# Fetching a and b from ScalarE's queue, moving one exact addition to VectorE, and a fixed order for an attention and rational-FFN kernel

## Chip, core and metric

The kernel runs on one core of one Trainium2 chip. The metric is the device time of one execution in microseconds (us), as the median of several executions. A core has five instruction streams: TensorE (PE in the profile, PEld for its weight loads), VectorE (DVE), ScalarE (ACT), GpSimd (POOL) and SyncE (SP), which here issues nearly all DMAs. Each works off its own list in the order in which it was written; they meet at semaphores.

## What is computed

Two softmax attentions run one after the other, and a feed-forward layer with a rational activation follows. Cut to what matters:

```python
def _attn_ref(q, k, v, p):                  # q, k, v: 8 x 8 x 576 x 64, p: 8 x 8 x 32 x 64
    p_packed = sm_attn(p, k, v)             # 32 packed rows ask 576 keys
    return sm_attn(q, p_packed, p_packed)   # 576 queries ask the 32 packed rows

def _moe_ref(x, w_in, w_out, a, b):         # x: 4608 x 512, w_in: 512 x 2048, w_out: 2048 x 512
    h = x @ w_in
    P = a[0] + a[1] * h + a[2] * h**2 + a[3] * h**3
    Q = 1.0 + abs(b[0]) * abs(h) + abs(b[1]) * h**2
    return (P / (Q + 1e-06)) @ w_out
```

w_in and w_out arrive as 64-bit floats. a holds four numbers and b two.

## The kernel before, in words

The work of the FFN is cut into 128 units: eight batches, each in two halves of 288 tokens, each of those with eight pieces of 256 hidden columns. For one unit TensorE makes two `h` tiles (weights folded with the packed attention in `m`, times the attention weights in `AH`), ScalarE makes three functions of each from PSUM (`Y`, `U`, `sq`), VectorE multiplies up the polynomial, GpSimd adds `U` and `sq`, ScalarE takes a logarithm and an exponential into `V`, VectorE joins them into `gh` (and `gl`), and TensorE adds their products with w_out into the two `acc` banks. The first twelve units and the whole first batch use plain 32-bit matmuls; later ones use split pairs.

Before a piece of weights can be used, its 64-bit words are turned into 32-bit floats. `convert()` does it for one pair of 512 KB transfers: two ScalarE ACTIVATEs of 128x1024, two VectorE bit operations (`TENSOR_SCALAR` and `SCALAR_TENSOR_TENSOR`, 128x1024) and one exact integer addition. That addition alternates between VectorE (even pairs, CUSTOM_DVE in the profile, ISA in the order) and GpSimd (odd pairs, TENSOR_TENSOR). Sixteen pairs are converted. Raw words lie in the buffers `m` and `w`, results in `win`, `w` and `half`.

`constants()` fetches a and b into the tile `ab` with two tiny broadcast DMAs on SyncE's queue, scales them into `abS`, and works out a square root in the tile `root`: about a dozen VectorE operations on 128x1, two ScalarE ACTIVATEs, and four loads of a number into a ScalarE register (TENSOR_LOAD). Units need these before their first `Y`, `U` and `sq`.

The kernel isn't written in the order in which it runs. Every operation goes into a list, and a `Planner` with costs for each operation and each hand-over sorts the list (`order()`, by `schedule()` run forwards and backwards in several rounds); `pin()` keeps the first transfers in the order in which they stand. In `idle()` the kernel also puts small filler matmuls (operand `zero`, 64x96, added into an open `acc` bank, line L288 in the profile) where the planner sees TensorE wait before 150 us of its own reckoning. So a change anywhere can move instructions on all engines.

Everything that the planner issues has line L291 in the profile; groups are told apart by the names of their tiles.

```python
(nc.gpsimd if converted % 2 else nc.vector).tensor_add(dst.bitcast(I32), hi, di)
```

Of the kernel before, what the change touches and what calls it, by code (L numbers as in the profile page):

```python
# [15 lines left out]
I32 = mybir.dt.int32  # L16
# [7 lines left out]
P = 128  # L24
# [3 lines left out]

S = 2.0**-40


class Planner:
# [26 lines left out]
    FIRST = {"tensor": 700.0, "vector": 800.0, "scalar": 2000.0, "gpsimd": 1400.0, "sync": 700.0}  # L59
    ROUNDS = 6  # L60
    SWITCH = 95
    SLACK = 60, 100, 150, 220, 300
    IN_FLIGHT = 8
# [4 lines left out]
    def __init__(self, nc):  # L68
        self.nc, self.ops, self.pinned = nc, [], 0

# [23 lines left out]
    def cost(self, engine, name, args, kwargs):  # L94
        if engine == "sync":
            return self.DMA_ISSUE
# [39 lines left out]
    def shares(self, engine, calls):  # L136

        if engine == "gpsimd":
            return True
        if engine != "vector":  # L140
            return False
        name, args, _ = calls[0]
        aps = [x for x in args if isinstance(x, bass.AP)]
        if any(x.space == PSUM for x in aps):
            return False
        wide = sum(self.columns(x) > 8 for x in aps[1:])
        return wide > 1 or name in ("tensor_scalar", "tensor_copy")

# [42 lines left out]

    def schedule(self, before, after, rank, back=0):

        n = len(rank)
        need = [len(x) for x in before]
        at, start, end = [0.0] * n, [0.0] * n, [0.0] * n
        soon = {e: [] for e in self.ENGINES}
        ready = {e: [] for e in self.ENGINES}
        free = dict.fromkeys(self.ENGINES, 0.0) if back else dict(self.FIRST)
        port = {"vector": 0.0, "gpsimd": 0.0}  # L200
        mode, landed, dma = None, [], 0.0
        for i in range(n):
            if not need[i]:
                heapq.heappush(soon[self.ops[i][0]], (0.0, rank[i], i))
        now = 0.0
        left = n
        while left:
            for e in self.ENGINES:
                while soon[e] and soon[e][0][0] <= now:
                    heapq.heappush(ready[e], heapq.heappop(soon[e])[1:])  # L210
                if free[e] > now or not ready[e]:
                    continue
                if e == "sync" and not back and len(landed) >= self.IN_FLIGHT and landed[-self.IN_FLIGHT] > now:
                    free[e] = landed[-self.IN_FLIGHT]
                    continue
                _, i = heapq.heappop(ready[e])
                left -= 1
                s = now
                if e == "tensor" and not back and self.modes[i] != mode:
                    s += self.SWITCH  # L220
                    mode = self.modes[i]
                if not back and self.shared[i]:
                    s = max(s, port["vector" if e == "gpsimd" else "gpsimd"])
                    port[e] = s + self.costs[i]
                start[i] = s
                end[i] = free[e] = s + self.costs[i]
                if e == "sync":
                    if back:
                        dma = max(dma, end[i]) + self.transfers[i]
                        end[i] = dma + self.DMA_START + self.DMA_END - self.DMA_ISSUE  # L230
                    else:
                        dma = max(dma, s + self.DMA_START) + self.transfers[i]
                        end[i] = dma + self.DMA_END
                        landed.append(end[i])
                for j in after[i]:
                    need[j] -= 1
                    f = self.ops[j][0]
                    way = self.WAY.get((f, e) if back else (e, f), self.PASS)
                    way += back * (way > 0)
                    at[j] = max(at[j], end[i] + way)  # L240
                    if not need[j]:
                        heapq.heappush(soon[f], (at[j], rank[j], j))
            now = min(
                t
                for e in self.ENGINES
                for t in ([free[e]] if ready[e] else [max(soon[e][0][0], free[e])] if soon[e] else [1e12])
            )
        return start, end

    def order(self):  # L250
        n = len(self.ops)
        self.costs = [self.price(*x) for x in self.ops]
        self.transfers = [self.transfer(calls[0][1]) if engine == "sync" else 0 for engine, calls in self.ops]
        self.shared = [self.shares(*x) for x in self.ops]
        self.modes = [self.mode(*x) for x in self.ops]
        before = self.edges()
        after = [[] for _ in range(n)]
        for i, x in enumerate(before):
            for j in x:
                after[j].append(i)  # L260
        first = self.schedule(before, after, list(range(n)))
        best = None
        for slack in self.SLACK:
            start, end = first
            for r in range(self.ROUNDS):
                s, e = self.schedule(after, before, [-x for x in end], slack)
                m = max(e)
                rank = [m - x for x in e]
                rank[: self.pinned] = range(-self.pinned, 0)
                start, end = self.schedule(before, after, rank)  # L270
                if best is None or max(end) < best[0]:
                    best = self.best = max(end), start, end
        self.end, self.start = best[0], best[1]
        self.deps, self.t0 = dict(enumerate(before)), best[1]
        return sorted(range(n), key=lambda i: (best[1][i], i))

    def pin(self):

        self.pinned = len(self.ops)

# [42 lines left out]
def attention_rational_ffn(  # L323
# [171 lines left out]
    def convert():  # L495
# [354 lines left out]
    M = {}  # L850
# [112 lines left out]
    def acc_block(u, i):  # L963
# [160 lines left out]
```

## Time and profile before

| | |
|---|---|
| median of 3 runs | 777.11 us (776.41 to 777.18) |
| the profiled execution's own time | 776.27 us |
| its span from first to last instruction | 774.5 us |
| PE, DVE, ACT, POOL busy | 740.3, 687.1, 653.0, 473.2 us |
| moved from and to memory | 56.03 MB |

The span is 1.8 us shorter than the profiled execution's time; that part lies around the instructions. Busy time is a mean over very different stretches: in the first 60 us weights, keys and queries come in and the first batch's attention runs; until about 150 us the remaining words are converted beside the first units; then comes a long even stretch, and an end of some 20 us. A row of a timeline gives start, duration, engine, line, operation, tiles written and read, and in brackets how long the engine sat idle before it and what ended that.

### The profile page before, as it was taken

To read this page: it belongs to the slowest core of one execution; us is meant where nothing else is said; L and a number is where in the kernel's file an instruction comes from. 1 tells how busy PE (TensorE), PEld (TensorE's weight loads), DVE (VectorE), ACT (ScalarE), POOL (GpSimd) and SP (SyncE) were. 2 spreads that over 40 slices of the span, in tenths; PEclk is the share of its full clock that TensorE was granted. 3 is DMA by queue.
4 is the path that set the end of the run, shared out by engine and by line. 5 is a ranking of instruction groups with operands and counts; after the bars stand their busy time and mean duration, and the time that the engine had idled before them with its cause. 6 is when DMAs were issued, how large, how long until landed. Compare 5 with 4: busy or idle time off the path is not lost.

```text
span 774.5 us, 14987 instructions
## 1 busy us (share of the span) xinstructions
PE 740.3 (96%) x5332; PEld 568.4 (73%) x5332; DVE 687.1 (89%) x1289; ACT 653.0 (84%) x1465; POOL 473.2 (61%) x456
## 2 busy tenths in 40 slices
PE   2779999999999999999999999999999999999997
PEld 2445554588778887778788887778788887868885
DVE  4899999998999889998999889998999889998863
ACT  5789988999887898889886898989887898898872
POOL 1143568876695557756686556755686556866663
PEclk9879999999999999999999999999999999999999
DMA  9992630204601155023701155023701141000001
GB/s 299 338 372 76 193 41 0 85 29 55 104 1 56 44 68 91 1 87 48 111 1 55 45 55 104 2 86 41 117 1 55 42 57 35 1 2 28 28 0 41
DMA packets 152171, 56.03 MB, mean 72 GB/s; under 512 B 122272, under 2 KB 141472, under 8 KB 152096
## 3 DMA queue, kind: packets, MB, share of 16 engines
q1 hardware_dynamic: 151856, 54.81, 31.0%
q8 instruction: 42, 0.69, 0.4%
q14 instruction: 33, 0.27, 0.1%
q10 hardware_dynamic: 240, 0.26, 0.1%
HBM read 45.62 MB, written 9.44 MB: 71 GB/s over the span
## 4 chain that ended last, share of the span: by engine, by line
PE 68%; DVE 16%; DMA 7%; ACT 4%; issue 2%; POOL 2%; SPq 1%; ACTq 0%; DVEq 0%; POOLq 0%
PE acc L291 35%; PE h L291 20%; PE at L291 12%; DVE Y L291 8%; DMA w<-in_moe_w_in_dram 2%; DMA m<-in_moe_w_in_dram 2%; DVE V L291 2%; DVE kx L291 2%; DVE m L291 2%; DVE small L291 2%; DMA w<-in_q_dram 1%; SPq L291 1%; ACT Y L291 1%; POOL gl L291 1%; DVE w L291 1%
## 5 line engine op out<-in xcount | busy, mean ns | idle before, releaser
L291 POOL TENSOR_TENSOR U<-U,sq 128x576 f32<-128x576 f32 x128 | 185.4, 1449 | 94.6 <-ACT sq L291 47.3
L291 PE MATMUL acc<-w,gh 128*128 128x512 f32 x736 | 235.7, 406 | 0.7 <-DVE G L291 0.4
L291 PE MATMUL h<-AH,m 128*128 128x288 f32 x1024 | 199.5, 317 | 4.0 <-DVE Y L291 3.5
L291 PEld LDWEIGHTS h<-AH,m 128*128 128x128 f32 x1024 | 161.2, 189 | 46.5 <-DVE Y L291 24.5
L291 POOL TENSOR_TENSOR gl<-Y,gh 128x512 fp32r<-128x512 f32 x116 | 150.3, 1296 | 45.0 <-ACT gh L291 22.8
L291 PEld LDWEIGHTS acc<-w,gh 128*128 128x128 f32 x736 | 132.6, 188 | 38.7 <-issue 9.1
L291 ACT ACTIVATE Y<-h,abS 128x288 f32<-128x288 f32 x256 | 127.5, 513 | 30.5 <-PE h L291 26.2
L291 PE MATMUL acc<-w,gl 128*128 128x512 f32 x384 | 149.3, 413 | 0.0
L291 DVE SCALAR_TENSOR_TENSOR Y<-Y,abS,V 128x576 f32<-128x576 f32 x128 | 103.2, 806 | 35.2 <-ACT V L291 34.9
L291 ACT ACTIVATE sq<-h 128x288 f32<-128x288 f32 x256 | 108.4, 425 | 29.0 <-PE h L291 15.7
L291 DVE TENSOR_TENSOR Y<-Y,h 128x288 f32<-128x288 f32 x256 | 111.0, 448 | 20.6 <-ACT U L291 7.6
L291 DVE SCALAR_TENSOR_TENSOR Y<-Y,abS,h 128x288 f32<-128x288 f32 x256 | 125.7, 507 | 2.2
L291 ACT ACTIVATE U<-h 128x288 f32<-128x288 f32 x256 | 101.9, 426 | 8.0 <-DVE V L291 7.0
L291 ACT ACTIVATE V<-U,one 128x576 f32<-128x576 f32 x128 | 98.7, 771 | 8.0 <-DVE Y L291 3.8
L291 DVE SCALAR_TENSOR_TENSOR V<-U,V 128x576 f32<-128x576 f32 x128 | 96.4, 753 | 0.0
L291 PE MATMUL h<-AL,m 128*128 128x288 f32 x448 | 96.3, 295 | 0.0
L291 DVE SCALAR_TENSOR_TENSOR Y<-V,Y 128x576 f32<-128x576 f32 x116 | 87.1, 751 | 1.4
L291 PEld LDWEIGHTS acc<-w,gl 128*128 128x128 f32 x384 | 71.8, 188 | 20.7 <-issue 6.8
L291 ACT ACTIVATE V<-V 128x576 f32<-128x576 f32 x128 | 85.0, 664 | 0.8
L291 ACT CAST gh<-Y 128x512 fp32r<-128x512 f32 x116 | 74.1, 638 | 7.4 <-DVE Y L291 6.9
L291 PE MATMUL acc<-half,gh 128*128 128x512 f32 x240 | 80.0, 411 | 0.0
L291 POOL COPY G<-Y 128x64 f32<-128x64 f32 x116 | 27.5, 237 | 76.7 <-DVE Y L291 70.5
(139 smaller groups left out, 1007.5 us busy)
## 6 DMA issues: line engine op xcount, KB each, us to landing
w<-in_moe_w_out_dram SPq DMA_DIRECT2D x16, 512.0 KB, 6.6
out_dram<-half SPq DMA_DIRECT2D x15, 512.0 KB, 3.0
nat<-in_k_dram SPq DMA_DIRECT2D x48, 144.0 KB, 3.8
nat<-in_q_dram SPq DMA_DIRECT2D x48, 144.0 KB, 4.3
nat<-in_v_dram SPq DMA_DIRECT2D x24, 256.0 KB, 3.4
m<-in_moe_w_in_dram SPq DMA_DIRECT2D x10, 512.0 KB, 6.9
w<-in_moe_w_in_dram SPq DMA_DIRECT2D x6, 512.0 KB, 8.7
nat<-in_k_dram SPq DMA_DIRECT2D x4, 512.0 KB, 6.4
```

The costliest lines, as they stand in the source:

```text
L291: getattr(getattr(self.nc, engine), name)(*args, **kwargs)
```

## The change

Three edits. The two transfers of b and a are issued first of all and by ScalarE (`nc.scalar.dma_start`), b before a. The exact addition goes to GpSimd for odd pairs from the fourth pair on (`converted > 2`); so the addition of the second pair moves to VectorE. And the planner's search is gone: the order of all 6,793 listed operations comes from a packed table, which the title of the change describes as an order for the first thirty units; `replay()` only works out start times, for the filler matmuls. The count of operations is the same, and apart from the two transfers and the one addition each stays on its engine.

```diff
+ORDER = (
+    "c-oD52Yggzy8d~mmovR&CX-~+Lr9MV0)#37g5oMz*A-UR4)=<8uexj7Vp|t?)$1R1uOfm9iiooGB7sPg5=bLGnIx0UB-4A#%(>qQ"
...
     def order(self):
...
-        first = self.schedule(before, after, list(range(n)))
...
-        return sorted(range(n), key=lambda i: (best[1][i], i))
+        low, high = np.frombuffer(zlib.decompress(base64.b85decode(ORDER)), np.uint8).reshape(2, -1).astype(int)
+        order = (np.cumsum(low + 256 * high) % 2**16).tolist()
...
+        self.start, self.end = self.replay(order, before)
...
+        return order
...
     def constants():
         nc.vector.tensor_scalar(zero, ident[:, 0:D], 0.0, None, ALU.mult)
-        nc.sync.dma_start(ab[:, 0:4], a.rearrange("(o n) -> o n", o=1).broadcast_to([P, 4]))
-        nc.sync.dma_start(ab[:, 4:6], b.rearrange("(o n) -> o n", o=1).broadcast_to([P, 2]))
         nc.vector.tensor_scalar(abS[:, 0:6], ab, S, None, ALU.mult)
...
-        (nc.gpsimd if converted % 2 else nc.vector).tensor_add(dst.bitcast(I32), hi, di)
+        (nc.gpsimd if converted % 2 and converted > 2 else nc.vector).tensor_add(dst.bitcast(I32), hi, di)
...
+    nc.scalar.dma_start(ab[:, 4:6], b.rearrange("(o n) -> o n", o=1).broadcast_to([P, 2]))
+    nc.scalar.dma_start(ab[:, 0:4], a.rearrange("(o n) -> o n", o=1).broadcast_to([P, 4]))
     for what in (2, "r", 3, "p", "k0", "k1", "qr", 4, "rv", "v0", "v1", 5, "q0", "q1"):
...
-    nc.pin()
     constants()
```

First place: ScalarE from its first instruction on, before the change. `m` are raw words, `win` converted ones, `kx` the transposed keys.

```order
L365 ACT_TABLE_LOAD
L291 ACTIVATE m_1_75<-m_1_75 128x1024
L291 ACTIVATE win<-m_1_75 128x1024
L291 ACTIVATE m_2_76<-m_2_76 128x1024
L291 ACTIVATE win<-m_2_76 128x1024
L291 ACTIVATE m_3_78<-m_3_78 128x1024
L291 ACTIVATE win<-m_3_78 128x1024
L291 COPY kx_1_87<-at_1_89 128x512
```

The same place after it; lines are 45 higher, since the table stands ahead of them.

```order
L410 ACT_TABLE_LOAD
L336 DMA ab<-in_moe_b_dram 128x2
L336 DMA ab<-in_moe_a_dram 128x4
L336 TENSOR_LOAD abS x2
L336 ACTIVATE root<-root 128x1 x2
L336 ACTIVATE m_1_75<-m_1_75 128x1024
L336 ACTIVATE win<-m_1_75 128x1024
L336 ACTIVATE m_3_78<-m_3_78 128x1024
L336 ACTIVATE m_2_76<-m_2_76 128x1024
L336 ACTIVATE win<-m_2_76 128x1024
L336 ACTIVATE win<-m_3_78 128x1024
L336 COPY kx_1_87<-at_2_92 128x512
```

Two transfers, the register loads and both ACTIVATEs on `root` now stand ahead of the first words; the last register load follows one row later. On VectorE nine operations on `root` and `abS` stand ahead of the first words, and three more between the words of the first pair.

Second place: VectorE at the end of the first batch's attention, before the change. `AH` is what the first `h` matmuls read, `w_4`, `w_5` and `w_6` are raw words, `Y` belongs to the first unit.

```order
L291 TENSOR_SCALAR abS<-root 128x1
L291 TENSOR_REDUCE small<-kx_1_87 128x18
L291 TENSOR_TENSOR kx_1_87<-kx_1_87,small 128x576
L291 TENSOR_SCALAR small<-small 128x18
L291 TENSOR_SCALAR w_4_118<-w_4_118 128x1024
L291 RECIPROCAL small<-small 128x18
L291 STREAM_TRANSPOSE AH_3_113<-kx_1_87 128x576
L291 TENSOR_TENSOR kx_1_87<-kx_1_87,small 128x576
L291 SCALAR_TENSOR_TENSOR w_4_118<-w_4_118 128x1024
L291 STREAM_TRANSPOSE AH_3_113<-kx_1_87 128x576
L291 TENSOR_SCALAR w_5_119<-w_5_119 128x1024
L291 TENSOR_TENSOR Y_1_127<-Y_1_127,h_1_129 128x288
```

The same place after it.

```order
L336 TENSOR_TENSOR kx_1_87<-kx_1_87,small 128x576
L336 TENSOR_REDUCE small<-kx_1_87 128x18
L336 TENSOR_SCALAR small<-small 128x18
L336 STREAM_TRANSPOSE AH_3_113<-kx_1_87 128x576
L336 RECIPROCAL small<-small 128x18
L336 TENSOR_TENSOR kx_1_87<-kx_1_87,small 128x576
L336 STREAM_TRANSPOSE AH_3_113<-kx_1_87 128x576
L336 TENSOR_SCALAR w_4_118<-w_4_118 128x1024
L336 SCALAR_TENSOR_TENSOR w_4_118<-w_4_118 128x1024
L336 TENSOR_TENSOR Y_1_127<-Y_1_127,h_1_129 128x288
```

No operation on `root` is left here, both operations on the words `w_4` stand behind the second transpose into `AH`, and `w_5` no longer follows it directly: `w_6` comes first, four rows later. SyncE issues the transfers of `w_6` ahead of those of `w_5` too.

Third place: TensorE around the first batch's units 13 and 14, before the change. `w_15` and `w_16` are converted pieces of w_out, the `at` rows the first of sixteen small matmuls for the second batch's `m`.

```order
L291 MATMUL h_27_292<-AH_3_113,m_8_211 128x288 x2
L291 MATMUL h_28_293<-AH_3_113,m_8_211 128x288 x2
L291 MATMUL acc_15_219<-w_16_266,gh_6_283 128x512
L291 MATMUL acc_16_220<-w_16_266,gh_6_283 128x512 x2
L291 MATMUL at_55_328<-win,ppT_2_144 32x512
L291 MATMUL at_56_329<-win,ppT_2_144 32x512
```

The same place after it.

```order
L336 MATMUL acc_15_219<-w_15_242,gl_5_275 128x512
L336 MATMUL acc_16_220<-w_15_242,gl_5_275 128x512
L336 MATMUL h_27_292<-AH_3_113,m_8_211 128x288 x2
L336 MATMUL h_28_293<-AH_3_113,m_8_211 128x288 x2
L333 MATMUL acc_16_220<-w_15_242,zero 64x96 x14
L336 MATMUL h_30_301<-AH_3_113,m_9_243 128x288 x2
L336 MATMUL h_29_299<-AH_3_113,m_9_243 128x288 x2
L333 MATMUL acc_16_220<-w_15_242,zero 64x96
L336 MATMUL acc_15_219<-w_16_266,gh_6_283 128x512
L336 MATMUL acc_16_220<-w_16_266,gh_6_283 128x512
```

Where real work stood between the `h` of two units, fourteen fillers stand now, and the products with `w_16` come one unit later. In the whole program there are 10 fillers in six groups before, and 21 in six groups after. Behind this, to the end of the program, the order of the operations differs too, by some places in each engine's list.

More of the change, by code (lines that the diff above doesn't have):

```diff
@@ L1 @@
-import heapq
-from collections import deque
+import base64
+import zlib
 from contextlib import ExitStack
@@ L68, in __init__ @@
     def __init__(self, nc):
-        self.nc, self.ops, self.pinned = nc, [], 0
+        self.nc, self.ops = nc, []
     def __getattr__(self, engine):
@@ L94, in cost @@
     def cost(self, engine, name, args, kwargs):
-        if engine == "sync":
+        if name == "dma_start":
             return self.DMA_ISSUE
@@ L190, in edges @@
         return edges
[L192 to L200, printed above, removed]
-        mode, landed, dma = None, [], 0.0
[L202 to L247, printed above, removed]
```

141 lines of the change are left out of this document (118 added, 23 removed).

## Prediction

> **What bounds the kernel now.** I read the windows first, then the chain of waits over the first 110 us, then the timelines of the engines that it names, then groups by tile. The windows give, for a stretch, the busy time (and instructions) of PE, PEld, DVE, ACT and POOL, TensorE's granted clock, the share of DMA time and GB/s:
>
> ```profile
> 0.00:60.00 60.00, 35.47 (x351) 22.68 (x352) 44.09 (x82) 42.68 (x79) 14.11 (x14) 0.89 1.02 331
> 60.00:150.00 90.00, 89.09 (x531) 47.33 (x531) 88.74 (x165) 82.33 (x174) 58.45 (x40) 1.00 0.28 73
> 150.00:750.00 600.00, 596.23 (x4364) 482.62 (x4363) 543.85 (x1027) 519.08 (x1196) 390.70 (x393) 1.00 0.26 48
> ```
>
> Three regimes are to be seen. To 60 us the DMA share is 1.02, every engine has gaps, and PE idles 24.5 us. From 60 to 150 us PE (89.1 of 90) and DVE (88.7) are both full. From 150 to 750 us PE alone is full, idle 600 - 596.23 = 3.8 us. No edit takes TensorE work away, so the time falls only by what TensorE waits: nearly all of it at the front, where the three edits are. The chain says who sets the front's end (start, duration, what):
>
> ```profile
> 4.22 8.96 DMA m<-in_moe_w_in_dram
> ...
> 35.75 8.85 DMA w<-in_moe_w_in_dram
> ...
> 47.98 8.52 DMA w<-in_moe_w_in_dram
> 56.51 4.05 DMA pn<-in_p_dram
> 60.57 0.69 DVE w L291
> ...
> 87.64 0.60 DVE gh L291
> ```
>
> It goes back through DMAs to 4 us and through VectorE alone from 60 to 88 us; only then does TensorE carry it. I trust the VectorE part. I doubt the DMA part, since its last link (keys of the packed queries, `pn`) feeds no `w` operation. For 30 to 45 us I take VectorE as the pace:
>
> ```profile
> 31.11 0.15 DVE L291 SCALAR_TENSOR_TENSOR root<-ab 128x1 f32<-128x1 f32 x1
> 31.18 0.17 DVE L291 TENSOR_SCALAR abS<-ab 128x6 f32<-128x6 f32 x1
> ...
> 41.03 0.69 DVE L291 TENSOR_SCALAR w<-w 128x1024 int32<-128x1024 int32 x1
> ...
> 43.09 1.21 DVE L291 SCALAR_TENSOR_TENSOR w<-w 128x1024 int32<-128x1024 int32 x1
> 44.22 0.77 DVE L291 STREAM_TRANSPOSE AH<-kx 128x576 f32<-128x576 f32 x1
> 44.91 2.50 DVE L291 TENSOR_SCALAR w<-w 128x1024 int32<-128x1024 int32 x1
> ```
>
> No row has a bracket, so VectorE waits for nothing, and TensorE's first `h` groups wait for its transposes into `AH`:
>
> ```profile
> 42.58 2.29 PE L291 MATMUL h<-AH,m 128*128 128x288 f32 x4 [0.23 <-DVE AH L291]
> 45.04 1.24 PE L291 MATMUL h<-AH,m 128*128 128x288 f32 x4 [0.17 <-DVE AH L291]
> ```
>
> **The change, part by part.**
>
> *root and abS leave 31 to 40 us.* Twelve tiny VectorE operations ran between the two rows above and 39.6 us. Their durations:
>
> ```profile
> L291 DVE TENSOR_SCALAR root<-root x5: 113/146/267, 32.4 to 37.4; 128x1 int32<-128x1 int32 x3, 128x1 f32<-128x1 f32 x2
> L291 DVE RECIPROCAL root<-root x2: 156/156/156, 36.6 to 38.9; 128x1 f32<-128x1 f32 x2
> ```
>
> Twelve at 0.15 us are 1.8 us of busy time. But neighbours overlap: 31.11 to 31.18 is a step of 0.07 us, which makes 12 x 0.07 = 0.8 us. I take 0.10 a step, nearer to the start-to-start row: **-1.2 us** (bounds -0.8 and -1.8). In their new place, the first microseconds, VectorE is idle, as the addition's rows below show.
>
> *The words `w_4` go behind the second `AH` transpose.* That takes another 0.6 (41.03 to 41.63, by the 0.69 row) and 1.13 us (43.09 to 44.22) out of the way of the second `h` group, which could start near 45.04 - 1.2 - 1.7 = 42.1 us. For VectorE it is only a delay: the work comes back at once. Since VectorE is full until 150 us, I count 0.
>
> *A lock at 44.91 us.* That TENSOR_SCALAR took 2.50 us instead of 0.69, beside this GpSimd addition:
>
> ```profile
> 44.44 2.41 POOL L291 TENSOR_TENSOR w<-w,w 128x1024 int32<-128x1024 int32 x1 [1.89 <-DVE w L291]
> ```
>
> It cost 1.8 us. After the change four operations on `Y` (which read PSUM) stand there, and the next words' TENSOR_SCALAR comes behind them. If these cover GpSimd's 2.4 us, all is gained; if they come early, half of the lock stays. I take half, **-0.9 us** (bounds 0 and -1.8).
>
> *The second pair's addition moves to VectorE.*
>
> ```profile
> 14.43 2.40 POOL L291 TENSOR_TENSOR win<-m,win 128x1024 int32<-128x1024 int32 x1
> 15.45 1.94 DVE L291 TENSOR_SCALAR m<-m 128x1024 int32<-128x1024 int32 x1 [1.67 <-ACT win L291]
> 18.68 1.22 DVE L291 CUSTOM_DVE_ANT_0 win<-m,win 128x2048 uint16<-128x2048 uint16 x1
> 21.35 0.42 DVE L291 TENSOR_REDUCE small<-acc 128x1 f32<-128x256 f32 x1 [1.44 <-PE at L291]
> ```
>
> It adds 1.2 us to VectorE and removes a lock of 1.94 - 0.69 = 1.25 us: 0. VectorE's idle 1.44 us before the first reduction covers it anyway; without that cover it would be +1.2.
>
> *SyncE's queue.* Two small issues leave it, and `w_6` goes ahead of `w_5`. With the DMA share at 1.02, bytes and not issues set the landing. On ScalarE this removes two waits:
>
> ```profile
> 42.01 1.14 ACT L291 ACTIVATE w<-w 128x1024 f32<-128x1024 f32 x1 [1.41 <-DMA w<-in_moe_w_out_dram]
> ...
> 44.68 1.16 ACT L291 ACTIVATE w<-w 128x1024 f32<-128x1024 f32 x1 [0.44 <-DMA w<-in_moe_w_in_dram]
> ```
>
> They are up to 1.85 us on ScalarE, but VectorE sets the pace behind it: 0 (bounds 0 and -1.85).
>
> *Fillers.* Eleven more. Pieces of one and of two fillers in the chain:
>
> ```profile
> 96.10 0.31 PE acc L288 x2
> ...
> 104.35 0.47 PE acc L288 x4
> ```
>
> One more filler costs 0.16 us; eleven make 1.8 us. Fourteen stand between the `h` of units 13 and 14, where real work stood: that TensorE has nothing ready there is what a TensorE ahead of VectorE looks like, so I count 0 (bounds 0 and +1.8).
>
> *The order behind unit 30.* Its places change, its work doesn't. TensorE's idle 3.8 us there could go or double; I take 0.
>
> *The sum* is made for the profiled execution, 776.27 us (774.5 of span, 1.8 around it): -1.2 - 0.9 = -2.1, so 774.2. The median, 777.11, lies 0.84 above that execution, and so the forecast is **775.0 us**. About 0.2% (1.55 us) is what a measurement of this kernel tells from no change; 775.0 is 0.27% down.
>
> **The rivals.**
>
> *ScalarE's queue stands behind a and b (slower).* Before, its first words needed only their own transfer:
>
> ```profile
> 0.73 1.28 ACT L365 ACT_TABLE_LOAD   x1 [0.73 <-PEq L1109]
> 5.87 1.10 ACT L291 ACTIVATE m<-m 128x1024 f32<-128x1024 f32 x1 [3.85 <-DMA m<-in_moe_w_in_dram]
> ...
> 16.09 0.59 ACT L291 COPY kx<-at 128x512 f32<-128x512 f32 x1 [0.67 <-PE at L291]
> ```
>
> Now two register loads and both `root` ACTIVATEs stand ahead of them, and these wait for nine VectorE operations, which wait for b and a. The waits of such transfers, in us to landing (last column):
>
> ```profile
> ab<-in_moe_b_dram SPq DMA_DIRECT2D x1, 1.0 KB, 8.8
> ab<-in_moe_a_dram SPq DMA_DIRECT2D x1, 2.0 KB, 6.7
> out_dram<-full ACTq DMA_DIRECT2D x2, 64.0 KB, 2.5
> ```
>
> Issued at 2.0 to 2.5 us behind the table load, they land near 5 by the last row (ScalarE's queue, quiet memory) and at 9.2 to 11.3 by the first two (behind SyncE's full queue). The `root` chain takes some 2.4 us more (nine steps near 0.2 with their hand-overs, two ACTIVATEs), and six conversions at 1.1 take 6.6. Landing at 5 starts the words at 7.4 and ends them at 14, ahead of the copy at 16.09. From a landing at 7.1 on, each microsecond delays that copy and the attention behind it. At 11.3 it is +4.2 less the 2.1 gained: +2.1, 779.2; at 9.2 it is +0.0. Against it: the first two rows are of a queue with many transfers ahead in it, and ScalarE's is empty. Chance 0.11.
>
> The Trainium skill ("DMA: Bandwidth & Descriptors", Queues, rings and completion order) says that each DMA engine takes packets in turn from the queues that have work. By that rule b and a pass SyncE's backlog and this rival falls away; no row before shows two queues under load.
>
> *TensorE, not VectorE, paces 60 to 150 us (no change).* PE's 89.1 of 90 speaks for it. Then the fillers cost their 1.8: -2.1 + 1.8, 776.8. Against it stands the chain, which is VectorE's to 88 us. Chance 0.20.
>
> *The DMAs pace the first 60 us, as the chain has it (no change).* Then whatever VectorE gains waits for bytes: 777.1. Against it: VectorE's unbracketed rows. Chance 0.09.
>
> *TensorE stays awake (faster).* The granted clock is the third figure from the end of these rows (0.50 and 0.66):
>
> ```profile
> 40.00:45.00 5.00, 4.26 (x12) 2.74 (x12) 5.00 (x10) 3.15 (x6) 0.85 (x2) 0.50 1.04 396
> 55.00:60.00 5.00, 4.81 (x33) 2.82 (x34) 2.88 (x7) 3.68 (x6) 2.57 (x2) 0.66 0.89 314
> ```
>
> At 0.50 four `h` matmuls took 2.29 us, at full clock 1.24 (rows above). If the denser front keeps the clock up at one of these places, about 1.1 us more is gained: 773.9; at both, 772.8. Against it: TensorE still waits for the same transposes and scores. Chance 0.15.
>
> The Trainium skill ("TensorE: Matmul & The Clock Gate", HAM oscillation) puts the limit at an idle gap of about 3.4 us, after which the clock is halved. By that rule gaps must shrink below it, not merely shrink; the five-microsecond means here can't show single gaps.
>
> **How the numbers follow.** The forecast's own case gets 0.45: 0.37 of it below 775.55 and 0.08 within 0.2%. The awake TensorE adds 0.15 to faster: 0.52. TensorE's pace gives 0.16 to same and 0.04 to slower (where the lock stays as well), the DMAs 0.09 to same, ScalarE's queue 0.11 to slower. Same 0.33, slower 0.15. The range begins where the upper bounds of root and lock and one warm place meet, -1.8 - 1.8 - 1.1 = -4.7: 772.4. It ends at 778.3, a little over the case in which the root step gains 0.8, the lock stays and all fillers count (+1.0, 778.1); most of ScalarE's rival is left outside.
>
> **What would show it.** Right: b and a landed by 6 us, the first word ACTIVATE at 7 to 8, the first reduction no later than 21.4, the second `h` group near 42, VectorE without idle time from 30 on, the fillers of unit 13 with no VectorE idle time beside them. The gain should stand at 88 us and stay to the end. Wrong: copies of `kx` later than 16.1 us, `AH` no earlier, a TENSOR_SCALAR of over 2 us again, or a gain at 90 us that is lost behind 150 us.

## The result, and the profile after

| | before | after |
|---|---|---|
| median | 776.38 us (775.79 to 777.18, 6 runs) | 782.33 us (780.15 to 783.15, 6 runs) |
| the profiled execution, span | 776.27, 774.5 us | 782.33, 780.5 us |

The ratio is 1.0079, with a 95% interval of 1.0063 to 1.0095: the change costs 6 us. The forecast was a gain, 775.0 us, with a range that ended at 778.3 us; the change went the other way.

The windows of the kernel after, with the same columns and bounds as before:

```profile
0.00:60.00 60.00, 28.23 (x338) 19.61 (x342) 36.30 (x72) 37.50 (x70) 8.79 (x12) 0.89 0.90 287
60.00:150.00 90.00, 87.63 (x518) 48.31 (x503) 87.78 (x167) 81.87 (x172) 49.30 (x36) 1.00 0.33 93
150.00:750.00 600.00, 595.82 (x4387) 477.03 (x4386) 540.92 (x1026) 520.83 (x1195) 395.67 (x396) 1.00 0.27 49
```

All engines did less in the first 60 us: PE 28.2 us of work instead of 35.5, VectorE 36.3 instead of 44.1, ScalarE 37.5 instead of 42.7. From 150 us on PE is as full as before (595.8 and 596.2). So the loss is made in the front and carried to the end. The DMAs give the first hint: 287 GB/s instead of 331. The window of 2 to 7 us, in the kernel before and in the kernel after (last two columns: DMA share, GB/s):

```profile
2.00:7.00 5.00, 0.00 (x0) 0.00 (x0) 0.00 (x0) 1.15 (x3) 0.00 (x0) 1.00 0.97 349
```

```profile
2.00:7.00 5.00, 0.00 (x0) 0.00 (x0) 0.31 (x2) 0.01 (x1) 0.00 (x0) 1.00 0.68 194
```

In these five microseconds, while b and a are on their way, the words and keys arrive at 194 instead of 349 GB/s. What that does to the engines, in the timelines of VectorE, ScalarE and TensorE of the kernel after:

```profile
5.31 0.16 DVE L336 SCALAR_TENSOR_TENSOR root<-ab 128x1 f32<-128x1 f32 x1 [3.77 <-DMA ab<-in_moe_b_dram]
...
9.48 0.17 DVE L336 TENSOR_SCALAR abS<-ab 128x6 f32<-128x6 f32 x1 [3.83 <-DMA ab<-in_moe_a_dram]
```

```profile
10.67 0.44 ACT L336 ACTIVATE root<-root 128x1 f32<-128x1 f32 x2 [8.65 <-DVE root L336]
11.04 1.10 ACT L336 ACTIVATE m<-m 128x1024 f32<-128x1024 f32 x1
...
19.43 0.59 ACT L336 COPY kx<-at 128x512 f32<-128x512 f32 x1 [0.48 <-PE at L336]
```

```profile
18.30 1.08 PE L336 MATMUL at<-ident,nat 128*128 128x128 f32 x4 [18.30 <-DMA nat<-in_k_dram]
...
50.38 2.62 PE L336 MATMUL h<-AH,m 128*128 128x288 f32 x8
```

b came at 5.3 us and a at 9.5. The first word ACTIVATE ran at 11.04 us (5.87 before), the first copy of `kx` at 19.43 (16.09 before). But TensorE's first row matters most: it does not wait for ScalarE; it waits for the keys themselves. In the kernel before it starts 3.3 us earlier:

```profile
14.96 1.09 PE L291 MATMUL at<-ident,nat 128*128 128x128 f32 x4 [14.96 <-DMA nat<-in_k_dram]
```

A second gap follows, in the timelines of ScalarE, VectorE and TensorE:

```profile
40.13 0.68 ACT L336 ACTIVATE kx<-kx 128x576 f32<-128x576 f32 x1 [0.33 <-DVE kx L336]
40.72 0.63 ACT L336 COPY m<-at 128x256 f32<-128x256 f32 x2
45.35 1.10 ACT L336 ACTIVATE w<-w 128x1024 f32<-128x1024 f32 x1 [4.01 <-DMA w<-in_moe_w_out_dram]
46.36 0.35 ACT L336 COPY m<-at 128x256 f32<-128x256 f32 x1
46.61 0.69 ACT L336 ACTIVATE kx<-kx 128x576 f32<-128x576 f32 x1
```

```profile
47.33 0.75 DVE L336 TENSOR_REDUCE small<-kx 128x18 f32<-128x576 f32 x1 [3.61 <-ACT kx L336]
```

```profile
48.62 1.76 PE L336 MATMUL at<-ident,nat 128*128 128x128 f32 x7 [6.12 <-ACT m L336]
```

The second exponential of the attention (`kx` at 46.61) and the last copies of `m` stand on ScalarE behind the words `w_4`, which are not needed yet and have not landed. ScalarE waits 4 us for them, VectorE 3.6 for ScalarE, and TensorE 6.1. Not all of it is `w_4`'s: VectorE had the second exponential's input ready at 43.7 us, so 2.9 us of its delay are. In the kernel before, the ACTIVATE on `w_4` stands ahead of the exponentials too, and waits for nothing:

```profile
35.94 1.23 ACT L291 ACTIVATE w<-w 128x1024 f32<-128x1024 f32 x1
```

### The profile page after: what moved, and what is told of

It is laid out like the page before. It is cut to its first block, busy times and chain, and to the rows that moved or that the text cites. A ratio compares the mean times of both kernels' runs of the same rounds, so it can differ in the third digit from the quotient of the medians.

```text
span 780.5 us, 15038 instructions
## 1 busy us (share of the span) xinstructions
PE 738.4 (95%) x5354; PEld 567.0 (73%) x5354; DVE 680.8 (87%) x1290; ACT 654.0 (84%) x1465; POOL 467.1 (60%) x455
## 4 chain that ended last, share of the span: by engine, by line
PE 82%; ACT 6%; DMA 4%; DVE 4%; POOL 1%; issue 1%; SPq 0%; DVEq 0%; ACTq 0%; POOLq 0%
PE acc L336 42%; PE h L336 24%; PE at L336 15%; DVE Y L336 3%; DMA nat<-in_k_dram 2%; ACT V L336 2%; DMA m<-in_moe_w_in_dram 2%; DMA w<-in_moe_w_out_dram 1%; ACT gh L336 1%; DVE V L336 1%; POOL U L336 1%; ACT sq L336 1%; ACT U L336 1%; SPq L336 0%; ACT Y L336 0%
## 5 line engine op out<-in xcount | busy, mean ns | idle before, releaser
L336 PE MATMUL acc<-w,gh 128*128 128x512 f32 x736 | 241.7, 407 | 3.9 <-DVE gh L336 1.5
L336 PE MATMUL h<-AH,m 128*128 128x288 f32 x1024 | 202.8, 315 | 1.9 <-DVE Y L336 1.8
L336 POOL TENSOR_TENSOR gl<-Y,gh 128x512 fp32r<-128x512 f32 x116 | 150.1, 1294 | 77.0 <-ACT gh L336 35.5
L336 PEld LDWEIGHTS h<-AH,m 128*128 128x128 f32 x1024 | 162.9, 189 | 42.1 <-DVE Y L336 20.9
L336 PEld LDWEIGHTS acc<-w,gh 128*128 128x128 f32 x736 | 134.2, 188 | 40.9 <-issue 10.3
L336 ACT ACTIVATE Y<-h,abS 128x288 f32<-128x288 f32 x256 | 129.1, 516 | 13.7 <-PE h L336 9.1
L336 DVE TENSOR_TENSOR Y<-Y,h 128x288 f32<-128x288 f32 x256 | 113.3, 447 | 25.1 <-ACT sq L336 12.9
L336 ACT ACTIVATE sq<-h 128x288 f32<-128x288 f32 x256 | 106.7, 418 | 20.9 <-PE h L336 13.3
L336 ACT ACTIVATE U<-h 128x288 f32<-128x288 f32 x256 | 104.7, 418 | 13.9 <-PE h L336 10.8
L336 ACT ACTIVATE V<-U,one 128x576 f32<-128x576 f32 x128 | 97.0, 758 | 18.1 <-DVE Y L336 9.6
L336 PEld LDWEIGHTS h<-AL,m 128*128 128x128 f32 x448 | 72.6, 188 | 1.1
```

The source lines that it names most:

```text
L336: getattr(getattr(self.nc, engine), name)(*args, **kwargs)
```

## The experiments

Three theories. T1: the two broadcast transfers slow all other transfers while they run. T2: ScalarE's queue stands behind the chain from b and a to `root`; this is the prediction's slower rival. T3: the table's order costs the time, a and b apart. And, for T3, the place: the words `w_4` in the front, or fillers, addition and the later order. To change single things, the planner's order of the kernel before was written down as a table too; that kernel has the same rows on all five engines as before. Ratios are to the kernel before, run on the same chip.

**The transfers alone.** In the kernel before:

```diff
-        nc.sync.dma_start(ab[:, 0:4], a...broadcast_to([P, 4]))
-        nc.sync.dma_start(ab[:, 4:6], b...broadcast_to([P, 2]))
+    nc.scalar.dma_start(ab[:, 4:6], b...broadcast_to([P, 2]))   # first on ScalarE's list
+    nc.scalar.dma_start(ab[:, 0:4], a...broadcast_to([P, 4]))
```

> The kernel before in every row, but for the two transfers of b and a, which leave SyncE's list and stand first on ScalarE's. The small operations on root and abS stay at 31 to 40 us, so nobody waits for b and a early. Theory T1 (the two broadcast transfers, 256 tiny packets at the head of the run, slow the DMA engines, so that words and keys land about 3 us later): first word ACTIVATE later than 5.87 us, first copy of kx at 18 to 19.5 us instead of 16.09, GB/s of the first 10 us near 212 instead of 271, time 779 to 782. Theory T2 (ScalarE's queue only waits for its head, the root chain): nothing waits, first copy of kx at 16.1, time 776 to 777. Theory T3 (the table's other order costs the time): 776 to 777 as well.

779.73 us, ratio 1.0048 (1.0032 to 1.0065). Window of 2 to 7 us and ScalarE's first rows:

```profile
2.00:7.00 5.00, 0.00 (x0) 0.00 (x0) 0.00 (x0) 0.01 (x1) 0.00 (x0) 1.00 0.69 184
```

```profile
9.61 1.10 ACT L336 ACTIVATE m<-m 128x1024 f32<-128x1024 f32 x1 [7.60 <-DMA m<-in_moe_w_in_dram]
...
20.22 0.59 ACT L336 COPY kx<-at 128x512 f32<-128x512 f32 x1 [1.13 <-PE at L336]
```

Nothing on ScalarE waits for b or a here, and still the words come 3.7 us late and the first copy 4.1 us late, later even than the 18 to 19.5 us that T1 expected. T1 holds; this part alone is worth 0.48%, 3.7 us.

**Without the transfers.** In the kernel after, two ScalarE copies from the identity tile stand in the transfers' place.

```diff
-    nc.scalar.dma_start(ab[:, 4:6], b...broadcast_to([P, 2]))
-    nc.scalar.dma_start(ab[:, 0:4], a...broadcast_to([P, 4]))
+    nc.scalar.copy(ab[:, 4:6], ident[:, 4:6])
+    nc.scalar.copy(ab[:, 0:4], ident[:, 0:4])
```

> The kernel after, with the two transfers replaced by two ScalarE copies of 128x2 and 128x4 from the identity tile; fetching a and b is left out. T1: words and keys land as before, first copy of kx at 16 to 16.5 us, time 775 to 777. T2: the root chain ends near 4 us, the words start near 6, and the time is also 775 to 777. T3: the table's order costs most of the loss by itself, time 780 to 782. If it comes below 775.5 the table's order gains what was forecast and the transfers alone cost it.

776.49 us, ratio 1.0018 (1.0004 to 1.0032): 0.61% of the 0.79% are gone. First copy of `kx` at 16.09 us, as before the change. Not all is back: ScalarE still waits 1.69 us for `w_4` in front of the second exponential.

**Words first.** In the kernel after, the transfers stay where they are; the `root` ACTIVATEs and register loads go behind the first six word ACTIVATEs.

```diff
  ScalarE: DMA b, DMA a
- TENSOR_LOAD abS x2; ACTIVATE root x2
  ACTIVATE m, win ... (six)
+ ACTIVATE root x2; TENSOR_LOAD abS x2
```

> The kernel after, with both transfers still at the head of ScalarE's list, but the two root ACTIVATEs and the register loads put behind the six ACTIVATEs of the first three pairs of words, and VectorE's root steps behind the first pair's and the second pair's additions. T1: the keys still land near 18 us, first copy of kx 18.5 to 19.5, time 780 to 782.5. T2: ScalarE's words start when they land, first copy of kx near 16.1, time 775 to 777. T3: no change, 781 to 783.

780.99 us, ratio 1.0074 (1.0057 to 1.0090), against 1.0079 for the kernel after. With nothing in front of it, the first word ACTIVATE runs no earlier:

```profile
11.16 1.10 ACT L336 ACTIVATE m<-m 128x1024 f32<-128x1024 f32 x1 [9.15 <-DMA m<-in_moe_w_in_dram]
```

T2 falls. In the kernel after, ScalarE's queue did stand behind b and a until 10.7 us, but here, where nothing stands in front of them, the words run at 11.16 us and not before the 11.04 us of that kernel: they had not landed earlier.

**The order alone.** In the kernel after, the transfers go back to SyncE and the `root` and `abS` operations to 31 to 40 us.

```diff
-    nc.scalar.dma_start(ab...)   # first; root and abS rows at the head of the lists
+    nc.sync.dma_start(ab...)     # behind the queries; root and abS rows where they stood before
```

> The kernel after, with the two transfers back on SyncE behind the queries' transfers and all root and abS operations back between the rows of 31 to 40 us, where they stood before; the table's other rows and the addition on VectorE stay. T1 and T2 alike: the front is as before, first copy of kx near 16.1, and the time shows what the rest of the change is worth without the early fetch: 775 to 777. T3: 780 to 782.

778.41 us, ratio 1.0035 (1.0022 to 1.0049), between the 775 to 777 that T1 and T2 expected and the 780 to 782 of T3. So the table costs 2.7 us without any early fetch, and 0.48% and 0.35% add up to the 0.79% of the change within their intervals. Its profiled execution is a long one (782.01 us). In it the second gap is there again, and SyncE's rows show where it begins:

```profile
28.19 2.76 SPq L336 DMA_DIRECT2D pn<-in_p_dram  x4
31.00 1.48 SPq L336 DMA_DIRECT2D AH<-in_q_dram  x1
33.59 1.88 SPq L336 DMA_DIRECT2D w<-in_moe_w_out_dram  x2
```

```profile
43.16 1.10 ACT L336 ACTIVATE w<-w 128x1024 f32<-128x1024 f32 x1 [3.54 <-issue]
```

The profile names no releaser for this wait; in the kernel after it named the transfer of `w_4`. The kernel before issued the same transfers at 28.44 us:

```profile
28.44 1.60 SPq L291 DMA_DIRECT2D w<-in_moe_w_out_dram  x2
```

**w_4 early.** The order alone, with `w_4`'s two issues moved up on SyncE:

```diff
  pn_2 x2
+ w_4 x2
  pn_2 x2, AH_2 (queries)
- w_4 x2
```

> The order-alone kernel (transfers on SyncE, root chain at its old place, the table's other rows kept) with one more edit: the two transfers of the words w_4 stand on SyncE's list behind the second of the four pn transfers, where they stood before, instead of behind all four and one of AH. Theory T3a (what the table costs is that w_4 lands late while its ACTIVATE stands on ScalarE ahead of the second exponential): ScalarE's wait of 3.5 us at 39.6 falls under 1 us, first h group near 44.5 instead of 48.2, time 1.5 to 3 us under the order-alone kernel, 775.5 to 777. Theory T3b (the table costs its time behind 60 us, by fillers, the moved addition or the later order): ScalarE's wait goes but the time stays at 777.5 to 779.

777.25 us, ratio 1.0018 (1.0004 to 1.0032). ScalarE's wait shrinks as expected, and `h` comes early:

```profile
37.48 1.12 ACT L336 ACTIVATE w<-w 128x1024 f32<-128x1024 f32 x1 [0.67 <-issue]
```

```profile
42.52 4.05 PE L336 MATMUL h<-AH,m 128*128 128x288 f32 x8
```

The ratio falls by half, in line with T3a, but its interval and that of the order alone overlap.

**At the head of SyncE.** The kernel before, with b and a first on SyncE's own list:

```diff
+ SyncE: DMA b, DMA a
  DMA m_1 x2, m_2 x2, AH, ...
```

> The kernel before with the two transfers of b and a moved to the head of SyncE's own list, ahead of the first words; all else as before. Theory T1a (256 tiny packets slow the DMA engines from whatever queue they come): GB/s of 2 to 7 us at 120 to 200 as with ScalarE's queue, first copy of kx at 19 to 20 us, time 779 to 781. Theory T1b (it is the second queue beside SyncE's that makes the engines share their time with tiny packets): behind one another in one queue the packets delay the words by the two issues, 1 us, and little more; first copy of kx near 17.5, time 776 to 777.5.

778.76 us, ratio 1.0043 (1.0024 to 1.0061), first copy of `kx` at 19.09. The time lies just under the 779 to 781 of T1a and far from the 776 to 777.5 of T1b: the second queue is not the cause. In one queue the cost has another shape, as the windows of 1 to 3 and 3 to 8 us and the DMA group show (KB, us to landing):

```profile
1.00:3.00 2.00, 0.00 (x0) 0.00 (x0) 0.20 (x1) 1.01 (x1) 0.29 (x1) 1.00 0.03 1
3.00:8.00 5.00, 0.00 (x0) 0.00 (x0) 0.00 (x0) 0.00 (x0) 0.00 (x0) 1.00 0.69 222
```

```profile
ab<-in_moe_a_dram SPq DMA_DIRECT2D x1, 2.0 KB, 4.6
```

From 1 to 3 us almost nothing moves: the DMA engines are busy 3% of the time, though the words are issued behind from 1.64 us on. So by this profile the engines are hardly at work on the tiny packets; that they wait for their data is the nearest reading, which no row shows.

**One packet each.** The transfers alone, but b and a go into one partition:

```diff
-    nc.scalar.dma_start(ab[:, 4:6], b...broadcast_to([P, 2]))
+    nc.scalar.dma_start(ab[0:1, 4:6], b...)      # ab is set to 1.0 before; a likewise
```

> The kernel with the transfers alone moved to the head of ScalarE's list, with one edit: b and a are read into one partition, one packet each instead of 128, and the other 127 rows are set to 1.0 by a VectorE memset of 128x6; the broadcast of a and b is left out. T1 (the number of packets): GB/s of 2 to 7 us back near 400, first copy of kx at 16 to 16.5, time 775 to 776. If it is the use of ScalarE's queue as such: 120 to 200 GB/s and 779 to 780 again.

774.88 us, ratio 0.9991 (0.9971 to 1.0011).

```profile
2.00:7.00 5.00, 0.00 (x0) 0.00 (x0) 0.00 (x0) 1.19 (x3) 0.00 (x0) 1.00 0.98 349
```

The rate is that of the kernel before, so ScalarE's queue as such costs nothing that can be measured.

**Other addresses.** The transfers alone, with as many packets of the same size, but from 128 places:

```diff
-    nc.scalar.dma_start(ab[:, 4:6], b...broadcast_to([P, 2]))
+    nc.scalar.dma_start(ab[:, 4:6], q[0, 0, 0:P, 4:6])      # a likewise, 0:4
```

> The kernel with the transfers alone moved to the head of ScalarE's list, with the same 256 packets of 8 and 16 bytes, but read from 128 different rows of q, 256 bytes apart, instead of one address; the values of a and b are left out. Theory T1c (the packets' number sets the cost): as with one address, GB/s of 2 to 7 us at 120 to 200, time 779 to 780. Theory T1d (all rows read one address, and those reads queue up in memory): GB/s near 350 to 400, first copy of kx at 16 to 17, time 775 to 777.

776.11 us, ratio 1.0008 (0.9993 to 1.0022). The window of 2 to 7 us and the two transfers:

```profile
2.00:7.00 5.00, 0.00 (x0) 0.00 (x0) 0.00 (x0) 0.85 (x2) 0.00 (x0) 1.00 0.98 343
```

```profile
ab<-in_q_dram ACTq DMA_DIRECT2D x1, 1.0 KB, 3.5
ab<-in_q_dram ACTq DMA_DIRECT2D x1, 2.0 KB, 4.7
```

Same queue, same 256 packets, same place in time: 343 GB/s from 128 addresses, 184 where all packets of a transfer read one. So it is not the number or the size of the packets that costs. That all of them read the same few bytes is what is left, with one thing not separated: the source is q here and no longer a and b. One packet from each of a and b cost nothing (the run before), but 128 reads of one row of q were not run.

**Root early and cheap.** The kernel before, with single packets spread by TensorE, and the whole `root` chain in the first 12 us:

```diff
+    tc.nc.scalar.dma_start(ab[0:1, 4:6], b...)          # a likewise
+    tc.nc.tensor.matmul(all_rows, ones, ab[0:1, :], start=True, stop=True)
+    tc.nc.vector.tensor_copy(ab, all_rows)
  root and abS rows: from 31 to 40 us to the head of ScalarE's and VectorE's lists
```

> The kernel before in its other rows, with b and a fetched at the head of ScalarE's list as one packet each into one partition, spread over the 128 partitions by one TensorE matmul with a row of ones and a VectorE copy of 128x6, and the whole root and abS chain done in the first 12 us (nine VectorE steps ahead of the first words, both root ACTIVATEs and the register loads behind the first two word ACTIVATEs). This tests the term of the prediction that took 1.2 us for the twelve small operations leaving 31 to 40 us. Theory A (VectorE sets the pace at 31 to 45 us): the second transpose into AH ends 0.8 to 1.8 us earlier relative to the first copy of kx, and the time is 0.8 to 1.8 us under before. Theory B (the front's end is set by transfers and by the clock): AH comes earlier, but the time is within 0.5 us of before.

775.81 us, ratio 0.9992 (0.9978 to 1.0007): no gain that can be measured. The profile shows why, in two places. The first is in the stretch that the twelve operations left:

```profile
15.45 0.59 ACT L336 COPY kx<-at 128x512 f32<-128x512 f32 x1 [0.63 <-PE at L336]
...
35.97 1.13 ACT L336 ACTIVATE w<-w 128x1024 f32<-128x1024 f32 x1 [1.30 <-DMA w<-in_moe_w_out_dram]
```

```profile
37.70 0.75 DVE L336 TENSOR_REDUCE small<-kx 128x18 f32<-128x576 f32 x1 [0.86 <-ACT kx L336]
...
43.67 0.77 DVE L336 STREAM_TRANSPOSE AH<-kx 128x576 f32<-128x576 f32 x1
```

From the first copy of `kx` to the second transpose into `AH` it takes 28.2 us, and 28.1 in the kernel before (16.09 to 44.22). VectorE, rid of the operations, waits for ScalarE instead, and ScalarE for the transfer of `w_4`. That the transpose stands 0.55 us earlier is no gain of the edit: the first copy had come 0.64 us earlier, with the keys. The second place is a lead that is lost. TensorE's third unit starts at 54.89 us, 1.3 ahead of the kernel before (56.22), and then:

```profile
54.89 3.39 PE L336 MATMUL h<-AH,m 128*128 128x288 f32 x8
...
63.22 1.24 PE L336 MATMUL h<-AH,m 128*128 128x288 f32 x4 [0.66 <-DVE Y L336]
64.39 0.66 PE L336 MATMUL at<-kx,small 64*32 64x256 f32 x16
```

The last row stands at 64.41 us in the kernel before. VectorE's row ahead of that wait, here and in the kernel before, and GpSimd's beside it here:

```profile
60.33 2.42 DVE L336 SCALAR_TENSOR_TENSOR w<-w 128x1024 int32<-128x1024 int32 x1
```

```profile
61.54 1.22 DVE L291 SCALAR_TENSOR_TENSOR w<-w 128x1024 int32<-128x1024 int32 x1
```

```profile
60.26 1.40 POOL L336 TENSOR_TENSOR U<-U,sq 128x576 f32<-128x576 f32 x1 [3.57 <-ACT sq L336]
```

The same VectorE operation starts 1.21 us earlier, takes 1.20 us longer, and both end within 0.01 us of each other. Now it runs beside GpSimd's addition of `U` and `sq`, and ends 1.09 us after it; before, that addition came at 62.40, in the operation's last 0.4 us. The lock at 44.91 us in the kernel before looks alike: there the VectorE operation ended 0.56 us after GpSimd's, and both figures are the operation's own time (1.22 and 0.69) less 0.13.

**Both mended in the table.** The kernel after, with single packets and `w_4`'s issues moved up:

```diff
  b and a: single packets and the TensorE matmul, as above
  SyncE: w_4 x2 behind the second pn_2
```

> The kernel after with two edits: b and a come as one packet each and are spread by a TensorE matmul, and the two transfers of the words w_4 stand behind the second pn transfer on SyncE's list. If the shared address and the late w_4 are the whole loss, first copy of kx near 16, ScalarE's wait ahead of w_4 under 1 us, first h group at 42 to 43, and the time is at or below before: 774 to 776.5. If the table loses behind 60 us too (fillers, moved addition, later order): 777 to 779.

776.61 us, ratio 1.0014 (0.9999 to 1.0028). The change's 6 us are reduced to 1, within what can be told from nothing. ScalarE still waits 1.67 us for `w_4`, where under 1 us was expected.

**No fillers.** That kernel without its fillers:

```diff
-FILL = {298: 2, 415: 1, 366: 2, 615: 1, 808: 14, 770: 1}   # which operation: how many ahead of it
+FILL = {}
```

> The kernel with single packets and the early w_4, without its 21 fillers; they add zeros, nothing else is left out. If TensorE is the pace from 60 to 150 us, each filler of 0.16 us counts: 2 to 3 us faster than with them. If they stand where TensorE waits anyway, no difference; if they keep the granted clock up, slower by 0.5 to 2 us.

776.22 us, ratio 1.0003 (0.9991 to 1.0014). Fillers cost nothing that can be measured: where fourteen stood, TensorE now waits the same time for VectorE. The rows with the fillers and without:

```profile
128.22 2.52 PE L333 MATMUL acc<-w,zero 128*64 128x96 f32 x28
```

```profile
129.27 3.24 PE L336 MATMUL h<-AH,m 128*128 128x288 f32 x8 [2.53 <-DVE Y L336]
```

**The addition alone.** The kernel before, with the second pair's addition on VectorE:

```diff
-        (nc.gpsimd if converted % 2 else nc.vector).tensor_add(...)
+        (nc.gpsimd if converted % 2 and converted > 2 else nc.vector).tensor_add(...)
```

> The kernel before with one edit: the second pair's exact addition runs on VectorE behind that of the third pair instead of on GpSimd. The prediction priced it at 0: 1.2 us more on VectorE, a lock of 1.25 us (TENSOR_SCALAR of 1.94 at 15.45 us) less, and 1.44 us of idle time ahead of the first reduction. Right: first reduction at 21 to 21.7 us, time within 0.5 us of before. Wrong: first reduction at 22 or later and 0.7 to 1.3 us slower.

775.67 us, ratio 1.0000 (0.9987 to 1.0014), first reduction at 21.64 us with 1.23 us of idle time still ahead of it. The price of 0 was right.

**w_4 behind the exponentials.** Root early and cheap, and ScalarE's and VectorE's work on `w_4` put off:

```diff
  ScalarE
- ACTIVATE w_4 (ahead of the exponentials), ACTIVATE w_8<-w_4 (behind the second)
  exp kx, COPY m x2, exp kx, COPY m x2
+ ACTIVATE w_4, ACTIVATE w_8<-w_4
```

> The early-root kernel (single packets, the root chain in the first 12 us, the other rows as before) with both ACTIVATEs of the words w_4 moved behind the last copy of the first m pieces on ScalarE, and VectorE's two operations on w_4 behind the second transpose into AH. Theory D (in the early-root kernel the transfer of w_4, for which ScalarE waited 1.30 us ahead of the first exponential, took the place of VectorE's small operations): no wait of ScalarE ahead of the exponentials, second transpose into AH at 41 to 42 instead of 43.67 us, time 1 to 2.5 us under before: 773.5 to 775. Theory E (the work is only put off, TensorE or VectorE takes it back before 90 us): AH earlier, time within 0.7 us of before.

775.56 us, ratio 1.0002 (0.9985 to 1.0019). The time did not move. In its profile the keys landed late, with the first copy of `kx` at 17.11 us instead of 15.45, and the second transpose into `AH` started at 43.34 instead of 43.67. Counted from that copy, the transpose comes after 26.2 us instead of 28.2. Of these 2.0 us, VectorE's two operations on `w_4` (0.69 and 1.21 us), which now stand behind the transpose, make 1.9. So `AH` came earlier because work was put off, as E has it, and next to nothing is left for D; it is one profile.

**The table with all mended.** Single packets, `w_4` issued early, and its ACTIVATEs behind the last copy of the first `m` pieces:

```diff
  ScalarE: exp kx, COPY m x2
- ACTIVATE w_4
  COPY m, exp kx
- ACTIVATE w_8<-w_4
  COPY m
+ ACTIVATE w_4, ACTIVATE w_8<-w_4
```

> The table with single packets and the transfers of w_4 moved up, and with both ACTIVATEs of w_4 moved behind the last copy of the first m pieces on ScalarE. Theory H (their position on ScalarE costs the time): ScalarE's wait of 1.67 us at 35.6 goes, transposes into AH end near 41, time 1 to 2 us under the kernel with single packets and early w_4 (776.6): 774.5 to 775.5. Theory E: the time stays at 776 to 777.

775.78 us, ratio 0.9995 (0.9981 to 1.0009). With both the fetch and the place of `w_4` mended, nothing measurable is left of the change's 0.79%. The interval does not meet that of the order alone (from 1.0022) either, which had no early fetch: there it is the issue and place of `w_4`, with the early root beside them, that take the table's loss back.

**Exponentials first.** The kernel after, with that last edit alone:

```diff
  ScalarE: as in the diff above; b and a stay broadcast, w_4's transfers late
```

> The kernel after with one edit: both ACTIVATEs of w_4 stand behind the last copy of the first m pieces on ScalarE instead of ahead of the second exponential; the broadcast transfers stay. Theory H (of the loss, the part at 41 to 45 us is the wait of ScalarE for w_4 in the wrong place): the wait of 4.0 us goes from ahead of the exponential, first h group near 46.5 instead of 50.4, time 2 to 4 us under after: 778 to 780. Rival (the DMAs are late and everything behind them waits anyway): first h group earlier but the time within 1 us of after, 781 to 783.

780.79 us, ratio 1.0070 (1.0054 to 1.0086). The wait is gone and the first `h` group is 5.9 us earlier than in the kernel after, but the time gains hardly 1 us, with intervals that overlap:

```profile
44.48 3.29 PE L336 MATMUL h<-AH,m 128*128 128x288 f32 x8
```

The rival comes nearer here. ScalarE now works on `w_4` and `w_6` from 42.55 to 47.8 us, between `h` and the unit's `U`; that `U` starts at 48.72 instead of 52.55 us, 3.8 earlier. By the first products with w_out the lead is 3.1:

```profile
60.01 1.13 PE L336 MATMUL acc<-w,gh 128*128 128x512 f32 x2 [1.48 <-DVE gh L336]
```

In the kernel after, this row is

```profile
63.15 1.12 PE L336 MATMUL acc<-w,gh 128*128 128x512 f32 x2 [1.48 <-DVE gh L336]
```

Read against the spans, this row says how the front's lateness reaches the end. In the kernels with the table and its fillers it stands at 63.15 (after), 60.01 (exponentials first) and 55.52 us (all mended, below), and the spans are 780.5, 778.1 and 774.0: from this row on, all three need 717.4 to 718.5 us. The order alone (row at 62.42 us, span 780.1), without the transfers (56.57, 774.6) and both mended in the table (56.15, 775.2) need 717.7, 718.0 and 719.1.

```profile
55.52 1.13 PE L336 MATMUL acc<-w,gh 128*128 128x512 f32 x2 [1.48 <-DVE gh L336]
```

None of the versions beats the kernel before by more than a measurement can tell; the best two that leave nothing out, root early and cheap (0.9992) and the table with all mended (0.9995), beat the changed kernel by some 0.8%.

## Why the prediction was wrong, step by step

**The step that failed first: what the two transfers cost.** The prediction asked when b and a land, and who waits for them. It had no term for what they do to the transfers beside them. That term is the largest of all: 0.48%, 3.7 us, with the rate at 184 instead of 349 GB/s from 2 to 7 us. The rival of the slower side had the right sign and place (copies of `kx` later than 16.1 us) but the wrong mechanism: a landed at 9.5 us, within its bounds, and ScalarE did stand behind it, yet freeing ScalarE (words first) did not bring the first word ACTIVATE forward (11.16 us against 11.04), because the words had been slowed as well. The bounds were met by luck: they assumed an issue at 2.0 to 2.5 us, behind the table load, but b and a were issued at 0.77 and 1.22 us, beside it, and took 4.5 and 8.2 us to land.

The prediction cited a rule of the Trainium skill ("DMA: Bandwidth & Descriptors", Queues, rings and completion order) by which b and a pass SyncE's backlog. The trace agrees for b, which landed 4.5 us after its issue, where it took 8.8 in the kernel before, and hardly for a, at 8.2 (6.7 before); from other addresses as many packets of the same size landed after 3.5 and 4.7. The rule says nothing of the shared address. Nearest to it is a row of the same page of the Trainium skill (Latency and other measured facts): with a row pitch of 4 MiB, copies fell to about half of their full rate by the pattern of addresses alone; the mechanism it gives is an inference that it calls unverified. Here the rate with one address was 184 GB/s and with 128 addresses 343; what happens in the memory is not shown by any run.

**SyncE's queue, priced at 0: the second failed step.** "With the DMA share at 1.02, bytes and not issues set the landing" looked at `w_5` and `w_6`. The table had also put `w_4`'s two issues behind two more `pn` transfers and one of `AH`; they were issued 5.2 us later in the order-alone run (33.59 against 28.44), and ScalarE, which meets `w_4` ahead of the second exponential, waited 3.5 us. An order listing shows both moves; each alone looked harmless. Early issue alone brought the order's 1.0035 to 1.0018; with single packets and the later place on ScalarE as well it was 0.9995.

**root and abS, -1.2 us: not there.** Early and cheap, the chain is worth -0.08% (-0.22 to +0.07), -0.6 us with zero inside. That VectorE had no idle time from 31 to 45 us was read rightly; the step that failed is to take that for the pace. Without the twelve operations VectorE waits 0.86 us for ScalarE, which had waited 1.30 us for the transfer of `w_4`, and the stretch to the second transpose is as long as before (28.2 and 28.1 us). This is the mechanism of the rival in which the DMAs pace the first 60 us. And the 1.3 us by which TensorE was ahead at 55 us, whatever brought them, were lost in a lock at 60.33 us, where the earlier VectorE operation met GpSimd.

**The lock at 44.91, -0.9 us: no gain.** In the mended table the next words' TENSOR_SCALAR, behind the four operations on `Y`, takes 1.10 us instead of 2.50: 1.4 of the 1.8 us of lock are gone, more than the half that was taken. But it no longer sets anything: VectorE waits 3 us for ScalarE ahead of these operations.

```profile
46.81 0.45 DVE L336 TENSOR_TENSOR Y<-Y,h 128x288 f32<-128x288 f32 x1 [3.03 <-ACT sq L336]
...
48.70 1.10 DVE L336 TENSOR_SCALAR w<-w 128x1024 int32<-128x1024 int32 x1
```

**Right:** the addition (1.0000), the fillers (776.22 without, 776.61 with), and the order behind unit 30, where TensorE's idle time is 4.2 us instead of 3.8. `w_4` behind the second `AH` transpose on VectorE was priced at 0; it was tried only together with ScalarE's part (`w_4` behind the exponentials), and there `AH` came 2.0 us earlier after the first copy of `kx` and the time stayed, which agrees. TensorE did not stay awake: the granted clock was 0.50 from 42 to 48 us, where it was idle but for 0.5 us (0.75 in the kernel before). The listed signs of a wrong forecast (copies of `kx` behind 16.1 us, `AH` no earlier) are what the profile shows.

## What to carry to other kernels

Price a small transfer by what it does to the transfers beside it, not only by when it lands. Here it helped to broadcast the few bytes on the chip (one packet and a matmul with ones); copies from different addresses cost nothing either. This was measured while the first big transfers run, and not elsewhere. When an order moves, follow the conversion that stands ahead of an exponential or a copy together with the issue of the transfer it waits for: a wait arises from both. Time taken off an engine without idle time is only won if the next lock or transfer is not already waiting to take it: an engine can be full and yet not set the pace.

## What the hardware showed that was not expected

- 128 packets of 8 bytes that all read b's address and 128 of 16 bytes that all read a's took the rate of all transfers from 349 to 184 GB/s for five microseconds. As many packets from 128 addresses of q, 256 bytes apart, left it at 343, single packets from b and a at 349.
- At the head of one queue such packets held it up: 1 GB/s and a DMA share of 0.03 from 1 to 3 us, and still 1 GB/s from 3 to 4 us, with the large transfers issued behind them from 1.64 us on. In the kernel before, these were issued from 0.73 us on and moved at 53 GB/s from 1.5 to 2 us.
- A VectorE operation on integers that started 1.21 us earlier, beside GpSimd's 1.40 us addition, took 2.42 instead of 1.22 us and ended at the same time, 1.09 us after GpSimd's.
